# A planned order with later-landing transfers, and earlier loads of x, in a two-block transformer kernel

## The chip, the cores and the metric

The kernel runs on one core of one Trainium2 chip. The metric is device time in microseconds (us) of one execution. Seven runs of the kernel before gave 1640.38 us as median, from 1637.94 to 1648.68 us.

## What is computed

The input x has 2048 tokens of 512 numbers. Twice in turn it goes through an attention block (32 heads of 16 numbers, no mask) and a feed-forward block of width 1376, each on a layer-normalised x, and each added to x. Cut to what matters:

```python
def attention(x, wqkv, wo):                 # A
    q, k, v = split(x @ wqkv)               # 32 heads of 16
    p = softmax(q @ k.T * 16 ** -0.5)       # 2048 x 2048 per head
    return concat(p @ v) @ wo

def ffn(x, w1, b1, w2, b2):                 # B
    return gelu(x_norm @ w1 + b1) @ w2 + b2

x = x + attention(layernorm(x)); x = x + ffn(layernorm(x))
x = x + attention(layernorm(x)); x = x + ffn(layernorm(x))   # the same weights again
```

Everything is bfloat16 at the borders.

## The kernel before

**Tiles.** x stays in SBUF as `xres`, 16 tiles of 128 tokens. The two attention blocks carry the numbers L = 1 and L = 3 in the code. Keys of all 2048 tokens lie transposed in `KT`, values in `V`. Queries are worked on in groups of 512 tokens; a segment is one group of queries with four heads. In the first block the first group of queries starts on the keys of tiles 0 to 3 alone (8 segments, "part 0"), while the other twelve tiles are still being projected; the rest of their keys follows as "part 1".

**Scores and exponentials.** A score tile is 128 keys by 512 queries of one head, one matmul of 32 contraction rows (line 1351). The exponential is taken in two places. ScalarE (ACT) takes groups of two or three score tiles at a time (line 1336; only groups of two before part 1 begins). VectorE (DVE) takes some of the tiles of five key blocks by arithmetic on the bits: one read of PSUM per tile (line 1428) and three shifted copies, made for two tiles at once where possible (line 1459). PE then multiplies the result with V (line 1525), four heads side by side. A tile that DVE takes costs PE four of these matmuls in place of one.

**Startup.** `build_startup` (line 666) writes the first transfers by hand: x tiles 0, 1 and 2 to 3 (`ldx`, line 672), then the weights of k, q and v, 512 KB each (`ldw`, line 675). All transfers go through the queue of SP, one after the other. `late()` (line 684) brings x tiles 4 to 15 as six transfers of two tiles (256 KB): tiles 4 to 7 once the keys of tile 3 have been stored, tiles 8 to 15 once the query transposes of the third segment have been issued. Tiles 0 to 3 go through `job_first_tile` (line 980), which transposes on PE. Tiles 4 to 15 go through `job_lnqkv` and `job_qkv_tile` (lines 846, 863): mean and variance (827, 828), the inverse root on GpSimd (835, 836), the normalised tile `xn` (840), a transposing DMA into `xnT` (874), then the projections on PE (897): first k and v of all twelve tiles, and q only once the norms of all keys have been issued. `xn` and `xnT` have three buffers each. Query rows go out to DRAM (1045 for the first four tiles, 952 later) and come back transposed as `qraw` (1100). Weights of the output projection `wo` (756) and the bias (752, 753) are loaded after the keys and values of all 16 tiles are under way.

**The order of the work.** No engine decides anything at run time: each runs a fixed list, in order, and waits on semaphores. The lists come from a planner in the file, which walks through a modelled time. Each operation is put forward as a task with a priority, a modelled duration, and for a DMA a modelled latency and bus time; `Prog.op` (line 104) computes its start `t0` and end `t1`, and the next task of an engine is the best one among those whose inputs are there (`Sched.best`, line 378). So a modelled landing time decides what is put ahead of what, and nothing else: data hazards are kept by the semaphores. For a DMA, `t1` is the issue time, plus issue duration, plus latency, and not before the shared bus is free (lines 118 to 124). The modelled numbers of the transposing DMA into `xnT` are 1.31 us for the issue and 1.2 us to land.

Where the planner leaves PE idle, `refill` (line 1155) goes through the plan again and puts matmuls of zeros (`zw`, lines 1260 to 1264) into the gaps, which keep PE busy and write nothing that is read.

## Time and profile before

| what | value |
|---|---|
| median of 7 runs | 1640.38 us |
| the profiled execution | 1643.78 us |
| its span, first to last instruction | 1642.0 us |
| PE busy | 1576.6 us, 96% of the span, zero matmuls included |
| ACT busy | 1557.5 us, 95% |
| DVE busy | 1491.9 us, 91% |
| POOL (GpSimd) busy | 378.3 us, 23% |
| DMA, hardware queue of SP | 17.1% of 16 engines' span |

The page has several parts. One gives the busy time of each engine; another cuts the span into 40 equal slices of 41.05 us and gives the busy share of each slice as a digit (9 is 90% or more), with the granted clock of TensorE in tenths of full speed. The view of groups sums instructions by line, engine and operation. The timeline lists instructions in order of time: start, length, engine, line, what is written from what, how many, and in brackets how long the engine had been idle before and who released it. "SPq" is the issue of a DMA on the queue of SP. The view of waits sums such idle times: total, how many, the longest. Stretches can be asked for by window, with the granted clock of each. DVE and POOL idle time costs nothing as long as nobody on the longest chain waits for them.

### The profile page before, as it was taken

How to read it: one execution, taken by the hardware profiler on the slowest of the kernel's cores; microseconds unless marked ns; L12 is line 12 of the kernel's file. 1: busy time of each engine (PE TensorE's matmuls, PEld its weight loads, DVE VectorE, ACT ScalarE, POOL GpSimd, SP SyncE). 2: the span in 40 equal slices, each digit the busy share in tenths (PEclk: the TensorE clock that was granted, in tenths of full speed). 3: DMA queues.
4: the chain of work that ended last, by engine and by line, in shares of the span. 5: the costliest groups of instructions: out<-in, count | busy, mean ns of one | idle time of the engine just before them, and what ended most of it. 6: DMA issues, size and time to landing. Idle time of an engine off the chain costs nothing.

```text
span 1642.0 us, 38723 instructions
## 1 busy us (share of the span) xinstructions
PE 1576.6 (96%) x16230; PEld 481.2 (29%) x16375; DVE 1491.9 (91%) x3282; ACT 1557.5 (95%) x1382; POOL 378.3 (23%) x575
## 2 busy tenths in 40 slices
PE   8999999999999999999999999999999999999998
PEld 3222222222222222222222222222222222344444
DVE  7779999979999999989999799999899999999894
ACT  6889999999999999989998999999999999999996
POOL 4345321112211022102102115411011101132220
PEclk9889999999999999999999999999999999999999
DMA  6562000103111021112712231010000000010000
GB/s 164 110 122 62 21 8 8 49 10 81 47 21 39 18 61 54 43 38 82 122 24 56 51 81 36 14 21 8 14 11 8 21 6 14 5 22 7 23 8 14
DMA packets 179119, 65.70 MB, mean 40 GB/s; under 512 B 158747, under 2 KB 173312, under 8 KB 178944
## 3 DMA queue, kind: packets, MB, share of 16 engines
q1 hardware_dynamic: 178944, 63.22, 17.1%
q8 instruction: 128, 2.10, 0.5%
q14 instruction: 47, 0.39, 0.1%
HBM read 19.96 MB, written 15.30 MB: 21 GB/s over the span
## 4 chain that ended last, share of the span: by engine, by line
PE 48%; DVE 30%; ACT 16%; issue 3%; DMA 2%; POOL 1%; SPq 0%; POOLq 0%; DVEq 0%
PE ps L1351 17%; ACT PT L1336 15%; PE ps L1525 14%; DVE dp L1428 11%; DVE dp L1459 8%; PE ps L1652 4%; PE ps L1690 4%; PE ps L897 3%; PE ps L1619 3%; PE ps L1260 2%; DVE accT L1555 2%; PE ps L1264 1%; DVE OT L1595 1%; DMA xnT<-xn 1%; ACT h L1682 1%
## 5 line engine op out<-in xcount | busy, mean ns | idle before, releaser
L1336 ACT ACTIVATE PT<-ps 128x1024 bf16<-128x1024 f32 (+1 forms) x1299 | 1479.1, 1254 | 58.3 <-PE ps L1351 51.5
L1351 PE MATMUL ps<-QT,KT 32*128 32x512 bf16 (+1 forms) x4608 | 680.3, 360 | 18.8 <-DVE dp L1428 6.7
L1428 DVE TENSOR_SCALAR dp<-ps 128x512 uint16<-128x512 f32 x881 | 590.2, 678 | 61.5 <-PE ps L1351 59.1
L1459 DVE TENSOR_SCALAR dp<-dp 128x1024 uint16<-128x1024 uint16 x1338 | 521.3, 429 | 9.2 <-PE ps L1525 4.7
L1525 PE MATMUL ps<-PT,V 128*17 128x512 bf16 (+1 forms) x3612 | 467.3, 359 | 0.1
L1525 PE MATMUL ps<-dp,vs 128*17 128x512 bf16 (+1 forms) x2988 | 426.8, 357 | 0.7 <-DVE dp L1459 0.5
L1128 POOL TENSOR_SCALAR vs<-V 128x340 bf16<-128x340 bf16 (+3 forms) x240 | 240.8, 1004 | 803.6 <-PE ps L1525 754.1
L1351 PEld LDWEIGHTS ps<-QT,KT 32*128 32x128 bf16 x4608 | 168.9, 91 | 557.4 <-ACT PT L1336 251.4
L1525 PE MATMUL ps<-dp,V 128*17 128x512 bf16 (+1 forms) x996 | 203.4, 359 | 3.2 <-DVE accT L1555 2.0
L1262 PE MATMUL ps<-zw 32*128 32x444 bf16 (+2 forms) x700 | 197.3, 326 | 0.0
L1264 PE MATMUL ps<-zw 128*32 128x448 bf16 (+25 forms) x1534 | 145.0, 324 | 0.5 <-DVE dp L1428 0.3
L1525 PEld LDWEIGHTS ps<-dp,vs 128*17 128x17 bf16 x2988 | 107.2, 88 | 123.9 <-issue 98.7
L1525 PEld LDWEIGHTS ps<-PT,V 128*17 128x17 bf16 x3612 | 111.2, 88 | 107.9 <-issue 96.3
L1260 PE MATMUL ps<-zw 128*128 128x448 bf16 (+17 forms) x510 | 121.2, 336 | 3.1 <-DVE ps L706 1.7
L1652 PE MATMUL ps<-yT,wf 128*128 128x512 bf16 (+3 forms) x358 | 94.6, 357 | 7.2 <-issue 4.1
L897 PE MATMUL ps<-wqkv,xnT 128*128 128x512 bf16 x301 | 90.2, 401 | 11.5 <-issue 3.3
L1619 PE MATMUL ps<-wo,OT 128*128 128x512 bf16 x207 | 60.3, 382 | 5.3 <-issue 3.8
L1676 DVE TENSOR_SCALAR h<-ps,b1c 128x512 bf16<-128x512 f32 (+2 forms) x88 | 62.0, 704 | 3.7 <-PE ps L1652 3.4
L1555 DVE STREAM_TRANSPOSE accT<-ps 128x512 f32<-128x512 f32 (+1 forms) x88 | 57.9, 658 | 7.3 <-PE ps L1525 6.9
L1525 PEld LDWEIGHTS ps<-dp,V 128*17 128x17 bf16 x996 | 48.4, 88 | 54.0 <-issue 27.6
L1260 PEld LDWEIGHTS ps<-zw 128*128 128x128 bf16 x510 | 39.7, 98 | 75.4 <-issue 45.9
L1264 PEld LDWEIGHTS ps<-zw 128*32 128x32 bf16 x1534 | 49.9, 95 | 23.5 <-issue 5.2
(172 smaller groups left out, 914.5 us busy)
## 6 DMA issues: line engine op xcount, KB each, us to landing
wf<-in_B_w_dram SPq DMA_DIRECT2D x90, 128.0 KB, 2.6
q_scr<-qk SPq DMA_DIRECT2D x22, 256.0 KB, 2.0
k_scr<-qk SPq DMA_DIRECT2D x12, 256.0 KB, 2.1
out_dram<-xres SPq DMA_DIRECT2D x16, 128.0 KB, 1.7
xres<-in_A_x_dram SPq DMA_DIRECT2D x7, 256.0 KB, 3.5
v_scr<-vst SPq DMA_DIRECT2D x12, 136.0 KB, 1.9
V<-v_scr SPq DMA_DIRECT2D x8, 204.0 KB, 4.4
wqkv<-in_A_wqkv_dram SPq DMA_DIRECT2D x3, 512.0 KB
```

Source lines behind the costliest of these rows:

```text
L897: yield Task("pe", prio, [I(lambda e, c=c: e.matmul(self.ps[:, b, :], lhsT=xnT[:, c, :], rhs=self.wqkv[:, c, which * 512:which * 512 + 512 ...
L1128: yield Task("pool", 0.8, [I(lambda e, k=k: e.tensor_scalar(out=self.vs[:, q, k - 1, i:i + n, :], in0=src, scalar1=WSHIFT[k], scalar2=None ...
L1260: fn = lambda e: e.matmul(self.ps[:, b, 0:w], lhsT=self.zw[:, 0:128], rhs=self.zw[:, 0:w], start=st, stop=st, skip_group_check=True)
L1262: fn = lambda e: e.matmul(self.ps[:, b, 0:w], lhsT=self.zw[32 * p:32 * p + 32, 0:128], rhs=self.zw[32 * p:32 * p + 32, 0:w], start=st, sto ...
L1264: fn = lambda e: e.matmul(self.ps[32 * p:32 * p + 32, b, 0:w], lhsT=self.zw[:, 0:32], rhs=self.zw[:, 0:w], start=st, stop=st, skip_group_c ...
L1336: S_.submit(Task("act", 1e-5 * gi, [I(lambda e, pt=pt, n=n, b0=b0: e.activation(out=self.PT[:, pt:pt + n, :], in_=self.ps[:, b0:b0 + n, :] ...
L1351: return [I(lambda e, kb=kb, i=i: e.matmul(self.ps[:, b, i * W:(i + 1) * W], lhsT=self.KT[32 * hp:32 * hp + 32, hg, kb * 128:(kb + 1) * 12 ...
L1428: self.S_.submit(Task("dve", 0.0, [I(lambda e: e.tensor_scalar(out=self.dp[:, u, w * 512:(w + 1) * 512], in0=self.ps[:, b, :], scalar1=BIT ...
L1459: yield Task("dve", pr, [I(lambda e, k=k, v=v: e.tensor_scalar(out=self.dp[:, v, 0:N], in0=self.dp[:, u, 0:N], scalar1=float(SHIFT[k]), sc ...
L1525: ops.append((nth[j, sh] + 0.1 * i, I(lambda e, hp=hp, v=v, ap=ap[:, i * W:(i + 1) * W], first=first and i == 0, W=W: e.matmul(self.ps[32 ...
L1619: yield Task("pe", pr, [I(lambda e, hg=hg, i=i, b=b: e.matmul(self.ps[:, b, :], lhsT=self.OT[:, hg, i * 128:(i + 1) * 128], rhs=self.wo[:, ...
L1652: yield Task("pe", pr, [I(lambda e, c=c: e.matmul(self.ps[0:M, b, off:off + W], lhsT=self.w1(fc, c), rhs=self.yT[:, c, 0:W], start=(c == 0 ...
```

## The change

Two edits. First, the modelled end of every DMA becomes 1.0 us later (`DMA_MARGIN`). The addition stands after the bus has been accounted for, so the modelled bus is occupied no longer than before; only those who wait for the transfer see it later. Second, x tiles 4 to 9 are loaded in `build_startup` by three transfers of two tiles directly behind the weights, and the late loader is left with tiles 10 to 15, all three behind the third segment's query transposes.

```diff
+DMA_MARGIN = 1.0
...
             if size:
                 self.bus = max(self.bus, op.t1 - size) + size
                 op.t1 = self.bus
+            op.t1 += DMA_MARGIN
...
         ldw(1, 512)
         ldw(0, 0)
         ldw(2, 1024)
+        for a in range(4, 10, 2):
+            ldx(a, a + 2)
+            self.S_.mark(("xld", a))
 
         def late():
-            yield ("keys", [("ks", 1, 3)])
-            for a in range(4, 16, 2):
-                if a == 8:
-                    yield ("keys", [("qraw", 2)])
+            yield ("keys", [("qraw", 2)])
+            for a in range(10, 16, 2):
                 yield self.dma(lambda e, a=a: e.dma_start(self.xres[:, a:a + 2, :], xr[:, a:a + 2, :]), [], [("x", a), ("x", a + 1)], 1.7, 0.5, (2.24, 1.04))
```

Because the planner's choices follow from each other, the lists of all engines come out in another order. What each list holds in total stays almost the same: 4608 score matmuls and the same DMAs in both, and these differences:

| instruction | before | after |
|---|---|---|
| DVE read of a score tile (1428) | 881 | 874 |
| DVE shifted copies, two tiles / one tile (1459) | 1305 / 33 | 1281 / 60 |
| ACT exponentials of three / two / one score tile (1336) | 617 / 682 / 0 | 619 / 682 / 1 |
| PE matmuls with V (1525) | 7596 | 7575 |
| PE matmuls of zeros: full, 32 rows, 32 columns (1260, 1262, 1264) | 510, 700, 1534 | 528, 709, 1762 |

In the text the line numbers are those of the kernel before; in the changed file the same lines stand up to three lines further down.

## The prediction, made before the changed kernel was run

> **What bounds the kernel now.** The page first, by engine and by slice:

> ```profile
> ACT  6889999999999999989998999999999999999996
> ...
> PEclk9889999999999999999999999999999999999999
> ```

> PE is 96% busy, but with zero matmuls among it; ACT has no filler and is 95% busy. So I read the span as ACT's work (1557.5 us) plus ACT's idle time (84.5), and ask of each edit which of the two it touches. The first three slices are ACT's worst outside the end, and there PE's clock also dips.

> Next the waits by window. ACT waits for scores 17.6 us from 0 to 125, 2.9 from 125 to 640, 22.2 from 640 to 1010, 7.5 from 1010 to 1470, 1.4 after that. The end has 11.2 more for the last feed-forward unit. Waits for DMA on any engine but POOL come to about 15 us before 125 and 2.0 us after it. So the edit on landing times has something to win only in the first 125 us; later it can only shuffle.

> The timeline of ACT shows two breaks there:

> ```profile
> 23.73 15.69 ACT L1336 ACTIVATE PT<-ps 128x1024 bf16<-128x1024 f32 x17 [1.93 <-PE ps L1351]
> 42.14 1.02 ACT L1336 ACTIVATE PT<-ps 128x1024 bf16<-128x1024 f32 x1 [2.72 <-PE ps L1351]
> 44.18 1.02 ACT L1336 ACTIVATE PT<-ps 128x1024 bf16<-128x1024 f32 x1 [1.02 <-PE ps L1351]
> 45.69 1.02 ACT L1336 ACTIVATE PT<-ps 128x1024 bf16<-128x1024 f32 x1 [0.48 <-PE ps L1351]
> 48.05 1.02 ACT L1336 ACTIVATE PT<-ps 128x1024 bf16<-128x1024 f32 x1 [1.34 <-PE ps L1351]
> ...
> 94.45 1.02 ACT L1336 ACTIVATE PT<-ps 128x1024 bf16<-128x1024 f32 x1 [3.23 <-PE ps L1351]
> ...
> 100.76 25.28 ACT L1336 ACTIVATE PT<-ps 128x1536 bf16<-128x1536 f32 x22 [2.27 <-PE ps L1351]
> ```

> The chain of waits says what PE itself waited for at both places, in time order:

> ```profile
> 34.46 5.17 DMA xnT<-xn
> ...
> 86.95 5.00 DMA xnT<-xn
> ```

> PE's list has projections (897) next, their transposed tile has not landed, and the scores stand behind them. PE stands still 2.04 us before 40.07 and 2.37 us before 92.39. These transfers land 2.5 us after issue in the median of all 40; these two took 5. And the gap is paid twice, as the windows show (length, PE, PEld, DVE, ACT, POOL busy, then the clock):

> ```profile
> 39.00:40.00 1.00, 0.00 (x0) 0.13 (x2) 0.96 (x2) 0.42 (x1) 0.00 (x0) 0.55 1.10 217
> ...
> 48.00:49.00 1.00, 1.00 (x6) 0.16 (x4) 0.62 (x2) 0.95 (x1) 0.21 (x2) 0.50 0.52 105
> 49.00:50.00 1.00, 1.00 (x12) 0.16 (x12) 0.80 (x2) 0.54 (x2) 1.00 (x2) 0.83 0.22 46
> ```

> The clock falls to half during the gap and stays there until about 49.4, some 10 us; the second time from about 90.3 to 100.5. PE is what bounds this stage, so half its clock is ACT idle.

> What held the first transfer is on SP's timeline:

> ```profile
> 27.14 2.47 SPq L1100 DMA_TRANSPOSE qraw<-q_scr  x2
> 29.65 1.09 SPq L689 DMA_DIRECT2D xres<-in_A_x_dram  x2
> 30.85 2.43 SPq L1100 DMA_TRANSPOSE qraw<-q_scr  x2
> 33.33 1.08 SPq L689 DMA_DIRECT2D xres<-in_A_x_dram  x2
> 34.46 4.65 SPq L874 DMA_TRANSPOSE xnT<-xn  x3
> ```

> Four loads of x and four query transposes stand ahead of it. The second has the weights of the output projection just ahead:

> ```profile
> 85.16 1.75 SPq L756 DMA_DIRECT2D wo<-in_A_wo_dram  x4
> 86.95 3.82 SPq L874 DMA_TRANSPOSE xnT<-xn  x3
> ```

> **The change part by part.** Besides the profile I use the order of both builds' instruction lists.

> *Loads behind the weights: 0.* SP issues nothing between 3.7 and 11.65 us; three issues of 0.42 to 0.5 us fit. The DMA engines are busy from 2 to about 8.6 us (235, 344, 362, 93 GB/s by windows of 2 us) and idle to 12. Three times 256 KB at 344 GB/s is 2.3 us, so they are through near 11, ahead of the first key transposes at 11.65. If that cover is gone, the key transposes come up to 2.3 us late, but the first scores wait for the longer DVE chain, which ends at 23.2.

> *First break: -5.* In the new list of SP no load of x stands between the four query stores. Before, two did (20.03 and 21.14), and the last store landed 4.12 us after 22.93, against 2.3 us in the median of these stores. So the query transposes go at about 25.3 in place of 27.14. Ahead of the first `xnT` stand two of them (2.47) and the three remaining x loads (1.65): it is issued at about 29.5, not 34.46. Its tile is normalised by then: mean and variance no longer wait for x (0.83 us at 24.03), and `xn` was made at 28.94 before. It lands at 32.0 (2.5 us) or, with three loads just ahead of it again, 34.7 (5.2 us). PE's list now asks for it after 26 score matmuls, not 34: four groups of two earlier, by 15.69 / 17 = 0.92 us each, at 34.3 in place of 38.0. So the gap lies between none and 0.4 us, against 2.04. ACT's idle time from 39.42 to 53.8 sums to 6.4 us, of which 0.8 is the stage's usual 0.21 per two exponentials; at most 5.6 goes, at least nothing if the clock falls all the same. I take 5.0, as the estimated gap is nearest to none.

> *Second break: -5.5.* The four loads of `wo` now stand behind two, and most of them behind three, of the `xnT` transfers; only the small bias loads remain ahead. Landing 2.7 us after issue (median of this window) instead of 5.0 takes 2.3 off, and PE's list has 14 scores ahead of the first of these projections, not 12: 0.97 us more cover. Together 3.3, against a gap of 2.37. ACT's idle time here is 3.23 + 0.48 + 0.48 + 2.27 = 6.5; I take 5.5, with 0 and 6.5 as ends. `wo` is first read at 253 us.

> *Start: +0.3.* In DVE's list, reads of x tiles 4 to 7 (827, 0.66 us each, 828 0.18) now stand inside the chain that makes the first query tile (1080, 1083, 1113), and behind them wait the first scores and so ACT. Two of them fall partly into waits that were there; up to 0.9 us is lost. Against that, on POOL the memsets of 735 and 736 (0.95 + 0.24) now stand ahead of the first 835 instead of between 835 and 836: up to 1.2 us won for the first tile, before DVE becomes the bound at 11 us. I take +0.3, ends -1.2 and +0.9.

> *More for ACT: +3.6.* The new plan gives DVE seven tiles fewer. By form an ACT instruction takes 1476 ns for three tiles and 1052 for two, so 2 x 1.476 + about 0.63 for the single one = 3.6 us. DVE saves 7 x 0.68 + 24 x 0.43 and pays 27 x about 0.3, some 7 us net, but has waited for scores (59.1 us) already; nobody gets that.

> *The rest of the order: 0, ends -6 and +6.* No row shows what a new order does after 125 us. The 22.2 us between 640 and 1010 are scores standing behind runs of feed-forward matmuls (3.46 at 732), or behind thin stretches: near 792 PE is under-occupied and the clock falls to half to 800. One such place more or fewer is worth about what the two above are, 6 us. The 255 additional zero matmuls fill planned gaps; 228 of them run four abreast.

> Sum: -5.0 - 5.5 + 0.3 + 3.6 + 0 = -6.6. The profiled execution took 1643.78 us around its span of 1642.0, and lies 3.4 above the median of the runs. 1643.78 - 6.6 = 1637.2; against the median, 1640.38 - 6.6 = **1633.8**.

> [...]

> **The rivals.**
> - *Only one break goes*: the first `xnT` again shares the DMA engines with three loads of x, now asked for 3.7 us earlier. If it takes over 5.2 us, PE stands, the clock falls, and -5.0 becomes about 0: 1638.8. For it: both slow landings had plain loads just ahead. Against it: 5 us are won on SP.
> - *Slower*: the clock falls at a new place in the change of blocks, as near 792 now, while the first break stays: 0 - 5.5 + 0.3 + 3.6 would be -1.6; with the second break also kept (a gap of over 1 us is enough, as the clock had fallen within about 1.3 us) it is +3.9, and a new half-clock stretch of 6 makes it 1650.3. It decides from the point where `xnT` lands more than 1 us after PE asks for it.
> - *The gain is larger*: the layer change loses one of its idle stretches, 6 us: 1628.
> - *It does nothing that counts*: gaps hidden anyway, same idle by another name: 1640.4.

> **How the numbers follow.** Forecast 0.45, larger gain 0.13, one break only 0.22, nothing 0.04, slower 0.16. A measurement here can tell about 0.3% from no change, 4.9 us: faster is below 1635.5. So faster 0.58, same 0.26, slower 0.16. The range goes from 1624 (all ends on the good side but for part of the rest) to 1646, which leaves out most of the slower case and the tail of the larger gain.

> **What would show it.** Right: no PE wait for `xnT` over 0.5 us before 125; clock 1.00 in slices two and three; the first `xnT` issued near 29.5; ACT idle before 125 about 10 us less; ACT busy 3.6 more. Wrong: a window at half clock near 35 to 45 or 90 to 100, the first exponential later than 24.6, or ACT's idle time after 640 grown by more than 6.

## The result, and the profile after

The changed kernel takes 1631.26 us in the median of 13 runs (1629.71 to 1639.72); the kernel before, run beside it, 1640.7 in 34 (1637.12 to 1648.68). The ratio is 0.9942, 95% interval 0.993 to 0.9954: 9.4 us faster, where 6.6 had been forecast. Its profiled execution took 1632.28 us around a span of 1630.5 (before: 1642.0).

In the changed file score tiles are read at L1431, exponentials are L1339, scores L1354, projections L900, `xnT` L877. The page of the kernel after, by slices:

```profile
ACT  6999999999999999989999999999999999999996
...
PEclk9999999999999999999999999999999999999999
```

The 8s of ACT in slices two and three are gone, and no slice has a clock under 0.9. One short stretch at half clock is new: the clock falls at 1002.5 us for 3.4 us, and ACT waits 1.43 us for scores behind it (before 1006.03). The timeline of ACT after, at the places of the two breaks (start, length, engine, line, what, how many; in brackets the idle time before and who ended it):

```profile
25.14 14.09 ACT L1339 ACTIVATE PT<-ps 128x1024 bf16<-128x1024 f32 x15 [2.77 <-PE ps L1354]
39.45 1.94 ACT L1339 ACTIVATE PT<-ps 128x1024 bf16<-128x1024 f32 x2 [0.21 <-PE ps L1354]
...
90.06 20.97 ACT L1339 ACTIVATE PT<-ps 128x1536 bf16<-128x1536 f32 x18 [0.48 <-PE ps L1354]
```

After 25.14 nothing above 0.48 us stands in brackets before 125. But the first exponential begins at 25.14, 1.4 us later than before (23.73). The queue of SP after:

```profile
26.16 2.47 SPq L1103 DMA_TRANSPOSE qraw<-q_scr  x2
28.67 1.60 SPq L692 DMA_DIRECT2D xres<-in_A_x_dram  x3
30.32 1.22 SPq L877 DMA_TRANSPOSE xnT<-xn  x1
...
79.55 2.50 SPq L877 DMA_TRANSPOSE xnT<-xn  x2
...
83.82 2.58 SPq L877 DMA_TRANSPOSE xnT<-xn  x2
86.46 0.57 SPq L759 DMA_DIRECT2D wo<-in_A_wo_dram  x1
```

The first `xnT` is issued at 30.32 in place of 34.46, and the first `wo` stands behind four transfers into `xnT` for the q projections that it stood ahead of (79.55 to 85.19). The first of these four is issued 7.4 us earlier than before (86.95), and PE begins to use it at 83.67 without a stop. The transfers into `xnT` between 28 and 125 us land 2.5 us after issue in the median and 4.1 at most (2.7 and 5.2 before). The 4.1 are those of the first one, which lands at 34.45; PE is ready for it at 36.07 and does not stop.

I split every profiled span into ACT's busy time, ACT's idle time before 125 us, and its idle time after that. Summed from the windows, for all kernels of this study (in order of their telling; "tiles" are the score tiles that DVE takes; the first exponential stands for the start):

| kernel | span | ACT busy (tiles) | idle to 125 | idle after | first exponential | median, ratio to before (95%) |
|---|---|---|---|---|---|---|
| before | 1642.0 | 1557.5 (881) | 27.6 | 56.9 | 23.73 | |
| after | 1630.5 | 1560.0 (874) | 17.7 | 52.7 | 25.14 | 1631.26, 0.9942 (0.993 to 0.9954) |
| e1, margin alone | 1635.7 | 1558.1 (878) | 20.3 | 57.3 | 24.69 | 1637.96, 0.9977 (0.9965 to 0.9988) |
| e2, loads alone | 1641.1 | 1559.6 (879) | 23.8 | 57.7 | 25.00 | 1641.14, 0.9999 (0.9984 to 1.0013) |
| e3, margin to 125 us | 1626.9 | 1557.4 (884) | 18.6 | 50.9 | 25.65 | 1628.13, 0.9913 (0.9893 to 0.9933) |
| e4, margin from 8 us | 1627.8 | 1558.1 (880) | 18.1 | 51.6 | 25.05 | 1626.63, 0.991 (0.9891 to 0.9928) |
| e5, gaps filled | 1638.7 | 1557.5 (881) | 24.8 | 56.4 | 23.52 | 1642.03, 0.9992 (0.9975 to 1.001) |
| e6, margin 8 to 125 us | 1635.9 | 1562.5 (872) | 16.6 | 56.8 | 23.67 | 1637.77, 0.997 (0.9959 to 0.9981) |
| e7, fewer zeros | 1636.7 | 1562.4 (872) | 16.7 | 57.6 | 23.86 | 1640.24, 0.9983 (0.9973 to 0.9993) |
| e8, margin on `xnT` | 1643.7 | 1563.8 (869) | 18.4 | 61.5 | 24.23 | 1639.47, 0.9991 (0.9977 to 1.0006) |
| e9, margin 0.5 | 1641.0 | 1563.0 (872) | 19.8 | 58.2 | 26.36 | 1640.48, 0.9994 (0.9981 to 1.0007) |
| e10, margin 2.0 | 1630.3 | 1558.8 (878) | 21.9 | 49.5 | 27.57 | 1630.7, 0.9937 (0.9914 to 0.9959) |
| e11, margin after 125 us | 1638.6 | 1559.9 (877) | 26.5 | 52.2 | 23.76 | 1640.4, 0.9988 (0.9976 to 1.0) |

### The profile page after: what moved, and what is told of

Same layout as the page of the kernel before. It is cut to its first block, busy times and chain, and to the rows that moved or that the text cites. A ratio compares the mean times of both kernels' runs of the same rounds, so it can differ in the third digit from the quotient of the medians.

```text
span 1630.5 us, 39202 instructions
## 1 busy us (share of the span) xinstructions
PE 1569.7 (96%) x16465; PEld 491.8 (30%) x16609; DVE 1484.8 (91%) x3278; ACT 1560.0 (96%) x1385; POOL 378.3 (23%) x575
## 4 chain that ended last, share of the span: by engine, by line
PE 42%; DVE 29%; ACT 25%; issue 3%; POOL 1%; DMA 0%; POOLq 0%; DVEq 0%
ACT PT L1339 22%; PE ps L1354 14%; PE ps L1528 11%; DVE dp L1431 10%; DVE dp L1462 7%; PE ps L1693 3%; PE ps L1655 3%; PE ps L1263 3%; PE ps L900 2%; PE ps L1622 2%; ACT h L1685 2%; DVE accT L1558 1%; PE ps L1267 1%; DVE st L830 1%; DVE QT L1116 1%
## 5 line engine op out<-in xcount | busy, mean ns | idle before, releaser
L1339 ACT ACTIVATE PT<-ps 128x1024 bf16<-128x1024 f32 (+1 forms) x1302 | 1481.5, 1265 | 42.1 <-PE ps L1354 36.4
L1354 PE MATMUL ps<-QT,KT 32*128 32x512 bf16 (+1 forms) x4608 | 670.9, 358 | 17.7 <-DVE dp L1431 6.0
L1431 DVE TENSOR_SCALAR dp<-ps 128x512 uint16<-128x512 f32 x874 | 585.8, 678 | 69.4 <-PE ps L1354 66.5
L1462 DVE TENSOR_SCALAR dp<-dp 128x1024 uint16<-128x1024 uint16 (+1 forms) x1341 | 516.5, 426 | 8.4 <-PE ps L1528 3.5
L1354 PEld LDWEIGHTS ps<-QT,KT 32*128 32x128 bf16 x4608 | 168.4, 91 | 541.3 <-ACT PT L1339 264.2
L1528 PE MATMUL ps<-dp,V 128*17 128x512 bf16 (+1 forms) x989 | 208.3, 358 | 2.1 <-DVE accT L1558 1.8
L1265 PE MATMUL ps<-zw 32*128 32x444 bf16 (+1 forms) x709 | 197.8, 325 | 0.1
L1267 PE MATMUL ps<-zw 128*32 128x448 bf16 (+26 forms) x1762 | 159.5, 322 | 1.2 <-DVE dp L1431 1.1
L1263 PE MATMUL ps<-zw 128*128 128x448 bf16 (+10 forms) x528 | 125.7, 335 | 4.0 <-DVE ps L709 1.7
L900 PE MATMUL ps<-wqkv,xnT 128*128 128x512 bf16 x299 | 84.6, 382 | 6.9 <-issue 3.9
L1267 PEld LDWEIGHTS ps<-zw 128*32 128x32 bf16 x1762 | 59.1, 95 | 27.5 <-DVE dp L1431 6.0
```

Source lines behind the costliest of these rows:

```text
L900: yield Task("pe", prio, [I(lambda e, c=c: e.matmul(self.ps[:, b, :], lhsT=xnT[:, c, :], rhs=self.wqkv[:, c, which * 512:which * 512 + 512 ...
L1263: fn = lambda e: e.matmul(self.ps[:, b, 0:w], lhsT=self.zw[:, 0:128], rhs=self.zw[:, 0:w], start=st, stop=st, skip_group_check=True)
L1265: fn = lambda e: e.matmul(self.ps[:, b, 0:w], lhsT=self.zw[32 * p:32 * p + 32, 0:128], rhs=self.zw[32 * p:32 * p + 32, 0:w], start=st, sto ...
L1267: fn = lambda e: e.matmul(self.ps[32 * p:32 * p + 32, b, 0:w], lhsT=self.zw[:, 0:32], rhs=self.zw[:, 0:w], start=st, stop=st, skip_group_c ...
L1339: S_.submit(Task("act", 1e-5 * gi, [I(lambda e, pt=pt, n=n, b0=b0: e.activation(out=self.PT[:, pt:pt + n, :], in_=self.ps[:, b0:b0 + n, :] ...
L1354: return [I(lambda e, kb=kb, i=i: e.matmul(self.ps[:, b, i * W:(i + 1) * W], lhsT=self.KT[32 * hp:32 * hp + 32, hg, kb * 128:(kb + 1) * 12 ...
```

## The experiments

The theory to be tried: the change earns its time at the two early breaks, by transposed tiles that are there when PE asks and by the clock that then stays up; behind 125 us it draws another order. The rivals: one edit does it alone; it is the order later that gains.

**e1, the margin alone** (the loads as before):

```diff
+DMA_MARGIN = 1.0
...
+            op.t1 += DMA_MARGIN
```

> The 1.0 us on every modelled transfer, loads of x as in the kernel before. SP's list still has four loads of x and four query transposes ahead of the first xnT, so it is issued near 34.5 us; PE's list asks for it after 32 score matmuls (34 before). Between the k/v and the q projections PE's list has 21 scores (12 before). Theory (two gaps of PE, each with its half clock, make the gain; the rest is shuffle): the first break stays (PE gap of 2 us or more, half clock to about 49), the second goes; ACT gets three tiles more (1.5 us) and starts 1.4 us later, as in the changed kernel. 1640.7 - 5.5 + 1.5 + 1.4 = 1638, give or take 5 for the rest of the order. Rival 'it is the modelled landing alone': as the changed kernel, 1631. Rival 'it is the loads alone': as before, 1641 or above.

The expected 1638 came out, but not for the expected reason: both half-clock stretches are gone, so with the margin alone the first break does not stay, as I had thought it would. SP's and PE's timelines of e1 around the first projection:

```profile
30.37 2.12 SPq L691 DMA_DIRECT2D xres<-in_A_x_dram  x4
32.59 3.08 SPq L1102 DMA_TRANSPOSE qraw<-q_scr  x2
35.72 3.88 SPq L876 DMA_TRANSPOSE xnT<-xn  x3
```

```profile
39.62 0.81 PE L899 MATMUL ps<-wqkv,xnT 128*128 128x512 bf16 x3 [0.16 <-issue]
```

All four loads stand ahead again, but no longer directly ahead, and the transposition goes out 1.3 us later than before (34.46). It lands 2.8 us after its issue and not 5.2, so at 38.53, 1.1 us sooner than before (39.63); and PE is ready for it at 39.46 and not at 38.03, though its list asks after two score matmuls fewer: ACT began 1.0 us later and stopped once for 1.29. Both together close the gap, to 0.16 us from 2.04. Small stops of ACT (1.29 before 33.42, 0.70 near 92) are spread over the stage. At the end ACT waits 14.2 us for the last feed-forward unit, 7.4 before, but elsewhere behind 125 us it waits less, and its later idle time is that of before within 0.5.

**e2, the loads alone:**

```diff
-DMA_MARGIN = 1.0
+DMA_MARGIN = 0.0
```

> The six tiles of x behind the weights, no margin in the plan. SP's list has two query transposes, two loads, two query transposes and one load ahead of the first xnT; PE's list asks for it after 28 scores; the output projection's weights come out behind the q tiles' first transposes (17 xnT ahead of them, 12 before). Theory: xnT is issued near 32.5 and lands between 35.0 and 37.7, asked for at 35.2, so the first break shrinks (0 to 2.5 us) and the clock may or may not fall; the second goes. Start as before (26 zero matmuls ahead of the first transposes). 1640.7 - 5.5 - (0 to 5.6) + 1.0 for two tiles = 1631 to 1636, give or take 5. Rival 'margin alone': 1641. Rival 'loads alone': 1631.

The two old breaks are gone here as well, but a new one stands behind them. Its chain of waits, then PE's timeline, then the windows (length, PE, PEld, DVE, ACT, POOL busy, clock, DMA share, GB/s):

```profile
97.88 5.82 DMA xnT<-xn
103.72 0.71 DVE xn L1567
```

```profile
105.07 0.38 PE L1354 MATMUL ps<-QT,KT 32*128 32x512 bf16 x1 [1.96 <-DVE dp L1431]
```

```profile
104.00:106.00 2.00, 0.93 (x6) 0.29 (x7) 2.00 (x7) 0.92 (x1) 1.09 (x3) 1.00 1.13 284
106.00:108.00 2.00, 2.00 (x24) 0.47 (x26) 1.84 (x5) 1.09 (x2) 0.00 (x0) 0.63 0.99 270
108.00:110.00 2.00, 2.00 (x12) 0.25 (x5) 0.99 (x4) 1.96 (x2) 0.00 (x0) 0.50 0.80 153
```

A transposition issued at 97.88, with weights and query stores just ahead of it on SP, takes 5.82 us. DVE wants to write into the buffer it reads from and waits 1.84 us; the read of a score tile stands behind that on DVE, PE waits 1.96 us for its bank, and 1.5 us later the clock is at half (from 106.53). It is a different queue from the one the prediction looked at, but the same two-step price. The 1631 to 1636 that I expected were missed. So each edit alone removes both old breaks in its profile, and neither gives the time: 4.2 us and nothing, against 9.4 for both. What they lack against the changed kernel is only in part the stage before 125 us: of 5.2 us between the spans of e1 and the changed kernel 2.5 are idle time there, and of 10.7 for e2 it is 6.1. The rest lies behind 125 us, where the later runs show how far orders differ.

**e3 and e4, both edits, the margin cut off on one side.** After 125 us the engines other than POOL had waited 2.0 us for transfers in all, so there it should only shuffle; and the hand-written loads ahead of 8 us should not need it.

```diff
-            op.t1 += DMA_MARGIN
+            op.t1 += DMA_MARGIN if op.t0 < 125.0 else 0.0     # e3
+            op.t1 += DMA_MARGIN if op.t0 > 8.0 else 0.0       # e4
```

> Both edits, but the margin only on transfers that the plan issues before 125 us. Lists of the first stage as in the changed kernel. Theory: both breaks gone as in the changed kernel, start 1.4 us late as there; after 125 us a different shuffle, with ten tiles more on DVE than the changed kernel (884 to 874), about 5 us less of ACT: 1627 to 1634. Rival 'the margin also helps after 125 us': ACT's idle time after 125 us rises by 5 or more against the changed kernel, 1636 or above.

> Both edits, but no margin on transfers that the plan issues before 8 us (the loads written out by hand). Theory of the late start: the margin on the first loads made the plan put 28 zero matmuls of PE ahead of the first tile's transposes, and PE reached these at 9.05 us in place of 8.24; with 26 again the first exponential begins near 23.7, not 25.1, so 1.4 us less. PE's list asks for the first xnT after 28 scores and has three loads and two query transposes ahead of it: first break gone. Some of the output projection's weights come out ahead of the q tiles' transposes again, so the second may come back in part. 1630 if it does not, 1636 if it does. Rival 'the start is late because DVE's list reads x early': the first exponential stays near 25.

Both are faster than either kernel of the case, 0.9913 and 0.991 of before. Before 125 us both are within 1.0 us of the changed kernel; what they have over it lies in ACT's busy time (2.6 and 1.9 us) and in its later idle time (1.8 and 1.1). One theory fell: I had put the late start down to the margin on the first loads, which makes the planner place 28 zero matmuls ahead of PE's first real work and not 26. e4 has 26 again and began at 25.05 all the same.

**e5, the kernel before with its two gaps filled.** Is it the gap that costs, or the clock behind it? Ten and twelve more zero matmuls go ahead of the first projection of k and v and the first of q:

```diff
+HOLD = {1: 10, 97: 12}
...
+        def hold(op):
+            if any(r[0] == "xnT" for r in op.spec[2]):
+                proj.append(op)
+                n = HOLD.get(len(proj), 0)
+                for _ in range(n):
+                    b = next((b for b in op.spare if b == MISCB or P.readers.get(("ps", b))), None)
+                    put(ACCB if b is None else b, "full", 0, FILL_MOST, b is not None)
...
             if op.eng == "pe":
                 fill(op)
+                hold(op)
```

> The kernel before, with ten more zero matmuls of 448 columns ahead of the first projection of k and v and twelve ahead of the first projection of q; nothing else is moved, so the transposed tiles still land late and PE still does no useful work in both places. In the runs of the kernel before so far, the mean granted clock of a run goes from 0.991 to 0.999 and its span follows it, about 1.3 us for each 0.001 (1645.2 us at 0.991, 1634.9 at 0.998). Theory: what the gaps cost is mostly the half clock behind them. Then both windows (40 to 50, 90 to 100 us) run at 1.00, the mean clock of the runs rises from 0.995 to 0.998 or more, and the median falls by 4 to 7 us to 1635 to 1638, although PE's gaps as such stay. Rival: the missing useful work is the cost, and the zeros only take its place or get in the way: 1641 to 1643, whatever the clock shows.

In both places the clock now stays at 1.00, as expected; the time does not fall, against the expectation. The profile shows why for the first break. ACT and PE of e5, and its chain:

```profile
74.88 1.94 ACT L1348 ACTIVATE PT<-ps 128x1024 bf16<-128x1024 f32 x2 [0.21 <-PE ps L1363]
79.81 2.00 ACT L1348 ACTIVATE PT<-ps 128x1024 bf16<-128x1024 f32 x2 [2.99 <-PE ps L1363]
```

```profile
78.84 0.60 PE L898 MATMUL ps<-wqkv,xnT 128*128 128x512 bf16 x2 [2.60 <-DMA xnT<-xn]
```

```profile
74.76 4.03 DMA xnT<-xn
```

Between the first break and 49.5 us ACT makes eight exponentials in e5 where it makes four in the kernel before: about 4 us are won. They last until 75. There PE, four groups ahead, reaches a transposed tile that SP could issue only at 74.76 (in the profile of before, whose order e5 keeps, SP issues from 60 to 77.6 with pauses of at most 0.3 us) and that takes 4.03 us; PE stops for 2.60, the clock falls again (to half, from 80.4 to 83.8), and at 85.6 both kernels have made the same number of exponentials. The second break's saving stays in this profile, and is the 3.3 us between the spans. In the runs the median of the mean clock is 0.9965 against 0.995 (0.998 had been expected) and the time 0.7 us less, with an interval that includes no change. That is the time its rival had named, but the profile does not bear the rival out: the time was won and then lost again. So here a held clock was worth its time only as far as the next transfer: the gain of the first break was given back. The changed kernel keeps it: from 20 to 96 us its PE has no stop over 0.3 us.

**e6 and e7, a combination, and the start.** e6 has both edits and the margin only between 8 and 125 us; e7 is e6 with at most 18 zero matmuls ahead of PE's first real work.

```diff
-            op.t1 += DMA_MARGIN
+            op.t1 += DMA_MARGIN if 8.0 < op.t0 < 125.0 else 0.0
...
-                    if w < FILL_LEAST or need(t0, t - op.t0) <= 0.0:
+                    if w < FILL_LEAST or need(t0, t - op.t0) <= 0.0 or (op is pes[0] and self.nfill >= 18):   # e7 only
```

> Both edits, with the margin only on transfers whose planned issue lies between 8 and 125 us. Theory: the margin works through the transfers of the first stage alone; outside of it it only reshuffles. Then this is as fast as the faster of the two kernels that leave it out on one side (1628.1 and 1626.6 us): 1624 to 1629, clock 1.000, no break at the first transposed tiles, first exponential near 25. Rival: what the two had won over the changed kernel (3.1 and 4.6 us) is luck of the order after 125 us; then this lands anywhere from 1625 to 1636, with the clock still at 1.000.

> As the kernel with the margin from 8 to 125 us, but with at most 18 zero matmuls ahead of PE's first real work in place of 26 (four more come behind the first four transposes); the lists are otherwise the same. Theory on the late start: in the first 8 us zero matmuls run slower than planned by an amount that differs between executions, and the 26 of them end after the first normalised tile is there (8.2 us), so the first transposes and all behind them are about 1.2 us late. Then the first transposes come at about 8.2 in place of 9.4, the first exponential at 23.8 to 24.2 in place of 25.0, and the median is about 1 us lower. Rival: the start of the chain is set by DVE and POOL, or the fewer zeros leave PE slow for longer so that the first projections are slower: first exponential unchanged within 0.2, time the same.

e6 has the least idle time before 125 us of all (16.6) and is still 11 us slower than e4 (1637.77 to 1626.63, or 0.997 and 0.991 of before), past even the 1636 of its rival. The rival is right in kind: what e3 and e4 had over the changed kernel was luck of the later order. Of the 8.1 us between the spans of e4 and e6, 4.4 are ACT's busy time (DVE takes 872 tiles, not 880) and 5.2 later idle time, less 1.5 before 125.

On the start, e4 and e6 have the same 26 zero matmuls. The timeline of PE in e4, then in e6:

```profile
1.73 7.81 PE L1263 MATMUL ps<-zw 128*128 128x448 bf16 x26 [1.73 <-DVE ps L709]
9.38 0.61 PE L993 MATMUL ps<-ident,dp 128*128 128x128 bf16 x8
```

```profile
1.73 6.68 PE L1263 MATMUL ps<-zw 128*128 128x448 bf16 x26 [1.73 <-DVE ps L709]
8.25 0.39 PE L993 MATMUL ps<-ident,dp 128*128 128x128 bf16 x4
```

26 zero matmuls take 6.38 to 7.94 us in the seven profiles that have 26. Instruction by instruction the trace shows why: in e6 they start 0.37 us apart until 5.0 us and 0.19 apart from then on; in e4 the spacing halves only at 7.3. The first normalised tile is there at about 8.2, so a late change of pace, here called a slow ramp, costs up to 1.3 us by these numbers. In e7 the zeros end at 7.49, ahead of that, and the first exponential came at 23.86: what the theory asked of it, but no sooner than in e6, whose ramp was quick. No time was won: e7 is 2.5 us slower than e6 in the median. Its lists are those of e6 but for the first groups of PE, and the profiles show one thing that differs. The windows of e6, then of e7:

```profile
670.00:672.00 2.00, 0.44 (x5) 0.22 (x3) 1.40 (x4) 1.87 (x2) 0.00 (x0) 1.00 0.34 66
672.00:674.00 2.00, 2.00 (x18) 0.42 (x16) 1.32 (x3) 0.46 (x1) 0.00 (x0) 1.00 0.10 33
674.00:676.00 2.00, 2.00 (x18) 0.51 (x10) 1.86 (x5) 2.00 (x3) 0.00 (x0) 1.00 0.10 33
```

```profile
670.00:672.00 2.00, 0.14 (x3) 0.02 (x1) 1.49 (x4) 1.96 (x2) 0.00 (x0) 0.95 0.04 4
672.00:674.00 2.00, 1.99 (x5) 0.52 (x6) 0.09 (x1) 0.00 (x0) 0.00 (x0) 0.50 0.00 0
674.00:676.00 2.00, 2.00 (x15) 0.24 (x13) 1.40 (x3) 0.60 (x1) 0.00 (x0) 0.70 0.19 66
```

The same instructions in the same order: a PE gap of 1.56 us in e6 leaves the clock at 1.00; in e7 one of 1.87 us goes with a fall to half, and ACT loses another 1.8 us from 670 to 680. Why e7's gap is longer more often (median clock of its runs 0.998, e6's 1.000) stays open.

**e8, the margin on the transfers into `xnT` alone.**

```diff
-            op.t1 += DMA_MARGIN
+            op.t1 += DMA_MARGIN if any(w[0] == "xnT" for w in writes) else 0.0
```

> Both edits, but the margin only on the transposing DMAs into xnT; all others have their earlier modelled landing. Theory: the margin earns its gain by letting PE ask later for the transposed tiles. Then no PE or ACT wait for xnT over 1 us is left between 30 and 125 us (the loads alone left one of about 4 us of ACT idle time near 106 to 114), mean clock 1.000, and 1626 to 1633. Rival: the order made by later landings of the other transfers (x, weights, queries) counts as well: the wait near 98 us of the kernel with the loads alone stays, or another place breaks, and 1636 to 1642.

Before 125 us the theory nearly holds: idle 18.4, no half clock, but one gap of 1.23 us for `xnT` where none over 1 us was to be left. The time is the rival's: DVE takes 869 tiles (ACT busy 6.3 us longer), and the later idle time is the longest of all. Its profile is its slowest run, with the clock at half from 774.5 to 792; its median run is 6 us shorter.

**e9 and e10, margins of 0.5 and 2.0 us.**

```diff
-DMA_MARGIN = 1.0
+DMA_MARGIN = 0.5     # e9
+DMA_MARGIN = 2.0     # e10
```

> Both edits with a margin of 0.5 us in place of 1.0. In the profiles so far ACT's idle time before 125 us is 27.6 us before, 23.8 with the loads and no margin, 20.2 with the margin and the loads as before, 16.6 to 18.6 in the kernels with both; the rest of the span (span less that idle time) goes from 1608 to 1625 us in kernels whose first stage is equally good, 1614 in the kernel before. Theory: the first stage is what the change buys, and everything behind it is a draw of the order. Half the margin puts two or three more transfers ahead of PE's asking than none: idle time before 125 us 17 to 21, no PE wait for a transposed tile over 1 us, mean clock 0.999 or 1.000. The instruction lists give DVE 872 score tiles (881 before), so ACT is busy about 1562 us. With the later idle time of the others (44 to 62) the span is 1623 to 1645, likeliest 1635. Rival: a margin of 0.5 is too little, an xnT break of the size of the one with no margin stays: idle before 125 us 22 to 25.

> Both edits with a margin of 2.0 us. Theory: PE asks still later for the transposed tiles, so no wait for them is left, clock 1.000; but 33 zero matmuls stand ahead of the first real work of PE in place of 26 to 28, which delays the first exponential by about 1 us (5 x 0.2) against kernels with 28; idle before 125 us 17 to 20. DVE gets 878 tiles, ACT busy about 1558; the rest is a draw: span 1620 to 1640, likeliest 1630. Rival: the larger margin starves PE of projections so that the stage of the first tiles becomes longer and ACT's groups of three start later: idle before 125 us over 21, or the weights of the output projection, which go ahead of four more transposed tiles than with 1.0, make a break near 90 us again.

PE waits for a transposed tile at most 0.4 us in e9 (DVE once 1.2) and, its weight loads counted in, 0.5 in e10. Idle time before 125 us is 19.8 and 21.9, 2.1 and 4.1 more than with 1.0, and in e10 past the 21 that its rival had named. Somewhat over half of that is the start: 29 and 33 zero matmuls take 8.03 and 8.84 us, and the first exponential comes at 26.36 and 27.57, 1.2 and 2.4 later than with 1.0. The rest is mostly idle time between 60 and 125 us. e10 is fast all the same, through the shortest later idle time; e9 is no faster than before, through 872 tiles and 58.2 us.

**e11, the control: the margin after 125 us alone, loads as before.**

```diff
+            op.t1 += DMA_MARGIN if op.t0 >= 125.0 else 0.0
```

> The kernel before with the margin only on transfers planned at 125 us or later, loads as before: the control to the other cuts. PE's list is the same as before in its first 1154 groups of instructions; the first stage, with both its breaks, is therefore the old one. DVE gets 877 score tiles (881 before), so ACT is busy about 1.5 us longer. Theory: the whole gain sits in the first stage and later landings behind it only draw another order. Then ACT's idle time before 125 us stays at 25 to 28 us, both half-clock stretches stay, and the rest of the span (span less that idle time) lies anywhere in the 1608 to 1625 seen so far: 1634 to 1652, likeliest 1643. Rival: later landings help behind 125 us as such (the rest is 1613.5 us in the mean of five kernels with the margin there, 1616.9 in six without): rest 1608 to 1612, span 1634 to 1639, with the two breaks still there.

Both breaks are there as before; the timeline of ACT in e11:

```profile
43.18 1.02 ACT L1338 ACTIVATE PT<-ps 128x1024 bf16<-128x1024 f32 x1 [2.42 <-PE ps L1353]
...
94.63 1.02 ACT L1338 ACTIVATE PT<-ps 128x1024 bf16<-128x1024 f32 x1 [2.77 <-PE ps L1353]
```

Idle time before 125 us is 26.5. The rest, span less idle time before 125 us, is 1612.1; theory and rival overlap there, so this run does not say whether later landings help behind 125 us as such. The six lists with the margin there on every transfer have rests of 1608.4 to 1621.1, mean 1613.3; the five different lists without it, or with it on `xnT` alone, 1608.3 to 1625.3, mean 1616.9. The two spread far more than they differ.

## Why the prediction was right, point by point

Profile against profile the sum was -6.6 and came out at -11.5 (span 1642.0 to 1630.5); median against median at -9.4.

- **First break, -5.0: right, -5.3** (idle from the first exponential to 60 us, 6.9 to 1.6). The transposition was issued at 30.32, not 29.5, and took 4.1 us, between the 2.5 and 5.2 that had been weighed. The tile was there at 34.45, 5.2 us sooner than before, and PE asked at 36.07, not 34.3, mostly because the start was 1.4 us late. It was not that luck that closed the gap: in e6, which started as early as the kernel before, the tile was there at 33.69 and PE used it from 35.56 without a stop.
- **Second break, -5.5: right, -6.1** (idle from 60 to 125 us, 8.9 to 2.8). The clearance was larger than read from the lists: `wo` stands behind four transfers and then five, not two and three. That it has to stand behind them is not shown: in e10 all four loads of `wo` stand ahead, the transfer takes 4.85 us again, and no break follows, as PE asks later.
- **The rival that only one break goes** did not happen: no `xnT` behind the three loads took over 4.1 us. With the loads alone (e2) a cousin of it did happen, through DVE, which the prediction had not looked at.
- **More for ACT, +3.6: right in kind, +2.5.** Over all kernels ACT's busy time goes from 1557.4 (884 tiles) to 1563.8 (869), about 0.4 us for each tile that DVE does not take.
- **Start, +0.3: mis-sized, +1.5** in the idle time before the first exponential, outside the bounds given (-1.2 and +0.9). The first exponential at 25.14 is also past the 24.6 that the prediction had named as a sign of being wrong; it was the only one of these signs that came. The reads of x inside DVE's chain, which I priced, add some 0.2: the chain is 1.27 us late before the first of them. 0.81 of that is PE's: 28 zero matmuls took 7.48 us in this profile, 26 took 6.67 in that of before, and the first transposes came at 9.05, not 8.24. Two zero matmuls at 0.19 us each are 0.4 of it, and belong to the change; the other 0.4 is the ramp: the spacing halves at 5.0 us in the profile of before and at 5.8 in that of after, a moment that lies anywhere from 4.4 to 7.5 in the seven profiles with 26. The 0.46 that come up between the transposes and the chain I have not traced. e6, with the same loads behind the weights, began at 23.67: they cost nothing there, as predicted.
- **The rest, 0 within 6: -4.2** of later idle time, inside its ends and mostly luck. The half-clock stretch of 6.8 us at 793 that before has is gone, and the one of 3.4 us at 1002.5 is new. Taken with ACT's busy time, the rests of the lists with a healed first stage (after, e3, e4, e6, e8, e9, e10) lie from 1608.3 to 1625.3 around the 1614.3 of before. The ends of this term should have been about -6 and +11 with the tiles counted in (the upper end is the profile of e8, 6 us above its median run; the next is e9 with +7), and no view of before could have said where in it the change would land; the tiles alone were to be read from the lists.

So the forecast was right for the reason given, with two errors of size: the start, and a draw that fell well. The gain is shown for the stage before 125 us: 27.6 us of idle time became 17.7, it is 16.6 to 21.9 in every kernel with both edits, and 26.5 in the control without them there. That the whole 9.4 us belong to the idea of the change is not shown: e6, e8 and e9 carry it too and are 5, 3 and 2 us faster than before, the last two within their intervals of no change.

The clock accounts for much of it. In 35 runs of the kernel before the mean clock goes from 0.991 to 0.999 and the span follows it (correlation -0.92), 1.27 us for each 0.001. The median run of before has 0.995, that of the changed kernel 1.000: 5 x 1.27 = 6.4 us go with the clock, an estimate from that slope, in which the gaps that bring the clock down are contained. The profile of before has 0.992 and is one of its slower runs, so the differences of the profiles are larger than those of the medians.

## What to carry to other kernels

A planner's order is as good as its modelled landing times where an engine stands first in line for a transfer; later landings, or earlier transfers, pay there. Here the earlier loads without the later landings brought the wait up again, some transfers on. Everything behind such a place is drawn anew by any edit, here with a spread of some 17 us from profile to profile (13 without the slow profile of e8): judge an edit by the stage it was made for and keep the best of several orders, as with e3 and e4 here, which take 0.991 of the time before. A filler that held the clock up gained, in the one trial here, only as far as the next transfer that was not there.

## What the runs showed of the hardware

**The eight longest stops of PE came with a fall of the clock, the 24 next did not.** The timelines of the thirteen profiles show 32 stops of PE of 1 us or more between 20 and 1600 us. The eight longest (1.71 in e9, 1.87 in e7, 1.93 and 1.97 in e11, 1.96 in e2, 2.04 and 2.37 in the kernel before, 2.60 in e5) each came with a fall to half a clock; the 24 others, up to 1.69 us (e10), did not. The border, between 1.69 and 1.71 us here, is about half of one such stretch. The prediction's own reading that over 1 us is enough does not hold here. The length of a stop is not all, though. The clock fell at 90.30 in the kernel before, when the stop of 2.37 us had lasted 0.3 us, so that stop can have kept it down but hardly brought it down alone. And five of the thirteen falls (793 in the kernel before, 1002.5 in the changed one, 246 in e4, 790 in e5, 774.5 in e8) have no stop of 1 us ahead of them; what brings those about stays open. Nor does a busy PE end it at once: from 40.07 on PE was busy almost without a break in the kernel before (7.93 of the 8 us from 40 to 48), and the clock came back at 49.3.
